# An inner Strassen level on four of the seven products of an output stage

What was changed: the last stage of a gated mixer kernel is a matrix product that already uses one level of Strassen's scheme. In three quarters of it, four of the seven products are split once more, and the attention output that feeds the stage is kept in fp16 instead of bf16. (Strassen's scheme makes a product of 2 x 2 blocks from seven block products in place of eight, at the price of sums of blocks before and after.)

## The chip, the cores and the metric

One core of a Trainium2 chip. The metric is the device time of one execution in microseconds (us), the median over several executions. Verdicts use ±2% as "same"; 95% intervals stand beside the ratios. The engines are PE (TensorE), PEld (its weight loads), DVE (VectorE), ACT (ScalarE), POOL (GpSimd) and SP (SyncE, which issues the DMA transfers here). PSUM (`psum_all` in the profile) is the memory that PE's matmuls write and that DVE and ACT read (L435 `psum_all<-arena`, 2425 matmuls before; L1297 on DVE, L296 on ACT: `arena<-psum_all`); the kernel uses it in pieces that it calls banks. `arena` is the kernel's buffer space.

## The reference, cut to what matters

```python
x = A_x                                                  # 1 x 2048 x 1024, bf16
g = sigmoid((x * gate_w).sum(-1, keepdims=True))
# A: attention over 8 positions at a distance of 2, 32 heads; then  o @ wo     (1024 -> 1024)
# B: gelu(x @ w_in), a spatial product over the sequence, then      (z1*gs) @ w_out   (1792 -> 1024)
return g * A + (1 - g) * B
```

The gate is folded into the two activations earlier in the kernel, so both final products are one contraction of 1792 + 1024 = 2816 = 22 chunks of 128 (14 gated gMLP chunks, 8 attention chunks), for 16 tiles of 128 tokens by 1024 columns. That contraction is the output stage.

## The kernel before: the parts that matter

Five helpers carry the argument: a product into a PSUM bank, the seven Strassen steps (a generator, so that steps can be interleaved), the loads of activations, their sums, and one "quad" (two token tiles by two column halves of 512, with 2 x 11 chunks).

```python
def product(bank, pairs, start, N=512):                         # L435: the matmuls
    n = len(pairs)
    for m, (lhsT, rhs) in enumerate(pairs):
        nc.tensor.matmul(bank[:, 0:N], lhsT, rhs, start=(start and m == 0), stop=(m == n - 1), ...)

def strassen(A11, A12, A22, S1, S2, S3, S4, B11, B21, B22, T1, T2, T3, T4, vs, c11, c12, c21, c22, ...):
    # ... bank roles X, Y, Z, V; bookkeeping cut
    product(X, pairs(A11, B11), True, N);  nc.scalar.copy(Y[:, n], X[:, n]);   yield
    product(V, pairs(S1, T1), True, N);    share(vs, V[:, n]);                 yield
    product(Y, pairs(S2, T2), False, N);   nc.scalar.copy(Z[:, n], Y[:, n]);   yield
    product(X, pairs(A12, B21), False, N); c11(X);                             yield
    product(Y, pairs(S3, T3), False, N)
    seed = nc.scalar.copy(V[:, lo], Y[:, lo]); c22(Y);                         yield
    product(Z, pairs(S4, B22), False, N);  c12(Z);                             yield
    # ... the last step in two halves for the last quad, cut
    product(V, pairs(A22, T4), False, N);  c21(V);                             yield

def load_act(i):
    d = act_slots[i % 3]
    for a in range(2):
        row = i + 8 * a
        for x in range(2):
            src = zg_d[row][:, NFH * x * P:NFH * (x + 1) * P].rearrange("p (k t) -> p k t", t=P)
            sync.dma_start(d[F16][x][:, 0:NFH, a, :], src)                     # 7 gated chunks, fp16
            sync.dma_start_transpose(d[BF][x][:, NFH:KOH, a, :], o_d[...])     # 4 attention chunks, bf16

def out_quad(i):
    # ... slots cut
    for k0, k1, dt in ((0, NFH, F16), (NFH, KOH, BF)):                         # sums split by type
        t = d[dt]
        sums4([s[q][:, k0:k1, :] for q in range(4)], t[0][:, k0:k1, 0], t[1][:, k0:k1, 0], ...)
    # ... c11, c12, c21, c22: copy or add into the output buffer and store
    run(strassen(A(0, 0), A(1, 0), A(1, 1), ...))

# the stage
out_sums_late()                   # the last of the weight sums
load_act(1)
for i in range(8):                # eight quads, one after the other
    if i + 2 < 8:
        load_act(i + 2)
    out_quad(i)
```

## Time and profile before

| | before |
|---|---|
| time, median of 3 (a fourth run came later) | 665.98 us (665.54 to 666.79) |
| PE busy, share of the span | 99% |
| output stage, first to last matmul | 526.6 to 659.8 us: 133.2 us |
| the same in halves (matmuls of 256 columns, a 512 counts as two) | 1232 |

How to read what follows. A page of the profile names groups of instructions by source line and engine, "out<-in". A timeline row is: start, length, engine, line, operation, "out<-in", count, and in brackets the idle time of that engine just before, with what ended it. A row of the chain of waits is: start, length, what. The lines of the kernel before that carry the bound are in the prediction.

### The profile page before, as it was taken

The page shows a single profiled execution, that of the slowest core. Times are in us where ns is not written, and L with a number is a line of the kernel's source. Part 1 is how long each engine was busy: PE and PEld are TensorE (multiplying, and loading weights), DVE is VectorE, ACT ScalarE, POOL GpSimd, SP SyncE. Part 2 cuts the span into 40 slices and gives each one's busy share as a digit, 9 for nine tenths or more (in the row PEclk, how much of TensorE's full clock was granted, in tenths as well). Part 3 has the DMA queues.
Part 4 walks back from the last instruction along what each step waited for, and adds up shares of the span by engine and source line. Part 5 has one row for each costly group of instructions (what it writes and reads, how often), then busy time and mean ns, then how long its engine had stood idle before and what let it go on. Part 6 is the DMA issues. An engine that isn't in the chain of part 4 may idle for free.

```text
span 662.9 us, 10747 instructions
## 1 busy us (share of the span) xinstructions
PE 656.5 (99%) x4194; PEld 316.7 (48%) x4194; DVE 451.8 (68%) x671; ACT 294.4 (44%) x621; POOL 6.2 (1%) x15
## 2 busy tenths in 40 slices
PE   9999999999999999999999999999999999999998
PEld 4544467444454555444444444444444444444444
DVE  2520889978998999898868766887679853333301
ACT  4544676565587577799653111121121122222221
POOL 1000000000000000001000000000000000000000
PEclk9999999999999999999999999999999999999999
DMA  9988663797585050259974568479645789533000
GB/s 217 185 211 224 130 152 90 189 217 188 129 202 162 1 155 1 64 159 250 236 214 157 128 158 168 119 212 279 97 121 142 163 176 214 120 96 98 32 33 33
DMA packets 229475, 98.16 MB, mean 148 GB/s; under 512 B 177440, under 2 KB 215728, under 8 KB 229424
## 3 DMA queue, kind: packets, MB, share of 16 engines
q1 hardware_dynamic: 229136, 97.27, 61.0%
q8 instruction: 33, 0.54, 0.4%
q10 hardware_dynamic: 288, 0.20, 0.1%
q14 instruction: 18, 0.15, 0.1%
HBM read 45.10 MB, written 36.61 MB: 123 GB/s over the span
## 4 chain that ended last, share of the span: by engine, by line
PE 96%; ACT 2%; DVE 1%; DMA 1%; issue 0%; ACTq 0%
PE psum_all L435 72%; PE psum_all L293 17%; PE psum_all L303 3%; PE psum_all L355 2%; DMA att_L<-band_d 1%; ACT arena L815 1%; PE psum_all L318 1%; ACT arena L363 0%; PE psum_all L491 0%; DVE arena L708 0%; DVE psum_all L506 0%; PE psum_all L225 0%; PE psum_all L822 0%; ACT L815 0%; DVE arena L713 0%
## 5 line engine op out<-in xcount | busy, mean ns | idle before, releaser
L435 PE MATMUL psum_all<-arena 128*128 128x512 bf16 (+5 forms) x2425 | 495.9, 367 | 1.3 <-DVE psum_all L506 1.2
L435 PEld LDWEIGHTS <-arena 128*128 128x128 f16 (+1 forms) x2425 | 237.1, 98 | 258.9 <-issue 2.7
L293 PE MATMUL psum_all<-arena 128*128 128x512 bf16 x512 | 114.8, 379 | 0.0
L293 PEld LDWEIGHTS <-arena 128*128 128x128 bf16 x512 | 48.5, 98 | 56.2 <-issue 0.2
L708 DVE TENSOR_TENSOR arena<-arena,att_A 128x2048 f16<-128x2048 bf16 (+1 forms) x44 | 73.3, 1705 | 0.3
L296 ACT CAST arena<-psum_all 128x512 bf16<-128x512 f32 x64 | 37.3, 586 | 50.9 <-PE psum_all L293 50.9
L581 DVE TENSOR_TENSOR arena<-arena 128x1024 f16<-128x1024 f16 (+3 forms) x31 | 18.9, 610 | 47.1 <-PE psum_all L435 36.2
L453 ACT COPY psum_all<-psum_all 128x512 f32<-128x512 f32 (+1 forms) x30 | 15.8, 527 | 76.8 <-PE psum_all L435 73.0
L815 ACT ACTIVATE arena<-psum_all 128x448 bf16<-128x448 f32 x64 | 34.1, 546 | 19.4 <-DVE psum_all L506 9.8
L1095 ACT ACTIVATE arena<-psum_all 128x512 bf16<-128x512 f32 x56 | 31.5, 600 | 20.9 <-PE psum_all L435 13.9
L506 DVE TENSOR_TENSOR psum_all<-psum_all,arena 128x448 f32<-128x448 f32 (+1 forms) x58 | 37.3, 661 | 4.5 <-PE psum_all L435 3.6
L583 DVE TENSOR_TENSOR arena<-arena 128x1024 f16<-128x1024 f16 (+3 forms) x31 | 18.7, 608 | 30.9 <-PE psum_all L435 17.7
L712 DVE TENSOR_TENSOR arena<-arena 128x2048 f16<-128x2048 f16 (+1 forms) x22 | 37.2, 1704 | 0.1
L477 ACT COPY psum_all<-psum_all 128x512 f32<-128x512 f32 (+2 forms) x30 | 15.6, 522 | 46.2 <-PE psum_all L435 45.2
L363 ACT CAST arena<-psum_all 128x1988 f16<-128x1988 f32 (+3 forms) x25 | 33.9, 1357 | 1.2 <-PE psum_all L355 0.4
L459 ACT COPY arena<-psum_all 128x512 f32<-128x512 f32 (+1 forms) x30 | 16.2, 544 | 36.9 <-PE psum_all L435 33.1
L464 ACT COPY psum_all<-psum_all 128x512 f32<-128x512 f32 (+1 forms) x30 | 15.9, 528 | 36.3 <-PE psum_all L435 35.6
L870 ACT ACTIVATE arena<-arena 128x896 bf16<-128x896 bf16 x32 | 30.4, 959 | 0.0
L582 DVE TENSOR_TENSOR arena<-arena 128x1024 f16<-128x1024 f16 (+3 forms) x31 | 18.4, 609 | 10.4 <-PE psum_all L435 10.3
L1297 DVE TENSOR_TENSOR arena<-psum_all,arena 128x512 bf16<-128x512 f32 x8 | 5.5, 691 | 29.3 <-ACT psum_all L477 29.3
L303 PE MATMUL psum_all<-arena 128*128 128x385 bf16 x128 | 23.0, 331 | 0.0
L584 DVE TENSOR_TENSOR arena<-arena 128x1024 f16<-128x1024 f16 (+3 forms) x31 | 18.5, 605 | 2.9 <-PE psum_all L435 2.9
(95 smaller groups left out, 404.6 us busy)
## 6 DMA issues: line engine op xcount, KB each, us to landing
arena<-v_d SPq DMA_DIRECT2D x8, 960.0 KB, 6.2
z_d<-arena SPq DMA_DIRECT2D x14, 512.0 KB, 4.7
arena<-z_d SPq DMA_DIRECT2D x14, 512.0 KB, 4.4
zg_d<-arena SPq DMA_DIRECT2D x56, 128.0 KB, 2.2
arena<-zg_d SPq DMA_DIRECT2D x32, 224.0 KB, 3.2
band_d<-arena SPq DMA_DIRECT2D x28, 248.5 KB, 4.6
arena<-in_A_wqkv_dram SPq DMA_DIRECT2D x16, 256.0 KB, 4.4
o_d<-arena SPq DMA_DIRECT2D x4, 1024.0 KB, 6.3
```

Source lines behind the costliest of these rows:

```text
L293: nc.tensor.matmul(ps[:], w[:, t, kt, :], xT[:, kt, 512 * c:512 * (c + 1)], start=(kt == 0), stop=(kt == KT - 1))
L296: nc.scalar.copy(dst[:, :, 256 * c:256 * (c + 1)], ps[:].rearrange("p (n e) -> p e n", e=2))
L303: nc.tensor.matmul(ps[:, 0:VP + 1], xT[:, kt, i * P:(i + 1) * P], wvp[:, kt, :], start=(kt == 0), stop=(kt == KT - 1))
L363: nc.scalar.copy(dst, src)
L435: nc.tensor.matmul(bank[:, 0:N], lhsT, rhs, start=(start and m == 0), stop=(m == n - 1), skip_group_check=True)
L506: last_add[0] = nc.vector.tensor_tensor(out[:, n], a[:, n], vs, ALU.add)
L581: first = nc.vector.tensor_tensor(s_out[0], a21, a22, ALU.add)
L708: lambda ws=ws, in0=in0, in1=in1: tt(p5[:, ws], in0[:, ws], in1[:, ws], ALU.mult)), False
L712: lambda a=p3[:, ws], b=p3[:, ws.start + 4:ws.stop + 4]: tt(a, a, b, ALU.add)), not n
L815: nc.scalar.activation(z2[:, i + 8 * a, ZC * c:ZC * (c + 1)], bank[:, 0:ZC], ACT.Gelu_apprx_tanh, accum_out=s1[:, 4 * n + c:4 * n + c + 1])
L870: return nc.scalar.activation(junk, src, ACT.Square, accum_out=(s2, s2h)[x][:, n:n + 1])
L1095: last_gelu[0] = nc.scalar.activation(z1s[:, f, a, :], bank[:], ACT.Gelu_apprx_tanh)
```

## The change

Intent: take matmul time out of a stage that is nothing but matmuls. Quads 0 and 1 stay. The other six are done two at a time (a "pair"); four of a pair's seven products (numbered 1, 7, 4 and 2) become Strassen products of two token tiles by 2 x 256 columns over ten of the eleven chunks, the eleventh plain, in two rounds of two interleaved products; the other three products (`rest`) stay plain. DVE pays with sums of weights and activations. The diff, cut to its core:

```diff
-    o_d = dpool.tile([S, D], BF, name="o_d")
+    o_d = dpool.tile([S, D], F16, name="o_d")
 ...
-        for k0, k1, dt in ((0, NFH, F16), (NFH, KOH, BF)):
-            t = d[dt]
-            sums4([s[q][:, k0:k1, :] for q in range(4)], ...)
+    def act_sums(i):
+        sums4(so_slots[i], *[act_block(i, x, a) for a in range(2) for x in range(2)])
 ...
+    raw_in = {xa: pair_slot(R_OFF + 22528 + 2 * SQ * n) for n, xa in enumerate(((0, 0), (1, 0), (0, 1), (1, 1)))}
+    a_of = {1: raw_in[0, 0], 4: raw_in[1, 0], 7: raw_in[1, 1], 2: s_in[0]}
+    def load_block(q, x, a):                       # two loads, each followed by a transposing load
+        d = raw_in[x, a]
+        for i in range(2):
+            load_tokens(2 * q + i + 8 * a, x, d[:, 0:NFH, i, :], d[:, NFH:KOH, i, :])
+    def pair_sum(q): ...                           # L1368: an outer sum, 2816 elements
+    def inner_sums(n, last=True, first=True):
+        ...
+            tt(s[:, 0], a21, a22, ALU.add)         # L1374, 640 elements
+            tt(s[:, 1], s[:, 0], a11, ALU.subtract)
+            tt(s[:, 2], a12, s[:, 1], ALU.subtract)
+            tt(a21, a11, a21, ALU.subtract)        # L1378
+    def inner(side, n, put):                       # mm: matmuls of 256 columns, L1391
+        mm(X, part(0, 0), w.b11, True);                 nc.scalar.copy(Y[:, h], X[:, h])        # L1397
+        mm(V, [s[:, 0, k] for k in k5], w.t1, True);    nc.scalar.copy(vs, V[:, h])
+        mm(Y, [s[:, 1, k] for k in k5], w.t2);          tt(Z[:, h], Y[:, h], vs, ALU.add)       # L1405
+        mm(X, part(KI, 0), w.b21, False, 0, 0);         put(0, 0, X[:, h])
+        mm(Y, part(0, 1), w.t3);                        tt(V[:, h], Y[:, h], vs, ALU.add)       # L1412
+        mm(Z, [s[:, 2, k] for k in k5], w.b22, False, 0, 1);   put(0, 1, Z[:, h])
+        mm(Y, part(KI, 1), w.t4, False, 1, 0);  mm(V, [], [], False, 1, 1)
+        put(1, 1, V[:, h]);  put(1, 0, Y[:, h])
+        # (a yield after each step cut)
+    def rest(q, m): ...                            # products 3, 5, 6, plain; adds and stores
+    def out_pairs():
+        for q in (1, 2, 3):
+            more = q < 3
+            run(inner(0, 1, keep_first), inner(1, 7, add_first(kept[2])))
+            ...
+            if more:
+                for xa in ((1, 1), (0, 1), (0, 0)):
+                    load_block(q + 1, *xa)
+            run(inner(0, 4, to_out(q)), inner(1, 2, add_first(kept[1])))
+            if more:
+                load_block(q + 1, 1, 0)
+                pair_sum(0)
+                inner_sums(7)
+            ...                                    # rest, with the other sums between its steps
 ...
-    load_act(1)
-    for i in range(8):
-        if i + 2 < 8:
-            load_act(i + 2)
-        out_quad(i)
+    for xa in ((1, 1), (0, 1), (0, 0), (1, 0)):
+        load_block(1, *xa)
+    act_sums(0)
+    out_quad(0, {})
+    ...                                            # inner weight sums, the first pair's sums, out_quad(1)
+    out_pairs()
```

The program text is not the order on an engine: a scheduler sets that when the kernel is built. The prediction read the built order.

## The prediction

> **What bounds the kernel now.** I read the page's busy shares and slices first, then the chain that ended last, then groups by shape in the output stage, then timelines of ScalarE, VectorE and the DMA queue around that stage's start.
>
> ```profile
> span 662.9 us, 10747 instructions
> ...
> PE 656.5 (99%) x4194; PEld 316.7 (48%) x4194; DVE 451.8 (68%) x671; ACT 294.4 (44%) x621; POOL 6.2 (1%) x15
> ...
> PE   9999999999999999999999999999999999999998
> ...
> DVE  2520889978998999898868766887679853333301
> ...
> PEclk9999999999999999999999999999999999999999
> ```
> TensorE (PE) is busy throughout at full clock; VectorE (DVE) is nearly full until slice 32 and then has two thirds free. The last eight slices are the output stage, the only one the change touches apart from some sums and loads made just ahead of it.
>
> The chain of waits from 370 us on, in order of time (start, length, what):
> ```profile
> 369.92 287.49 PE psum_all L435 x1332
> 657.41 2.42 PE psum_all L491 x22
> 659.82 0.02 issue
> 659.85 0.42 DVE arena L1314
> ```
> So 290 us of unbroken matmuls end the kernel: nothing is waited for, 1332 matmuls take 287.49 us, 0.2158 each, and 22 of 256 columns take 2.42, 0.110 each. Any matmul time removed here is won whole, and any bubble made here is lost whole.
>
> Where the stage begins, from ScalarE's timeline:
> ```profile
> 529.24 0.57 ACT L453 COPY psum_all<-psum_all 128x512 f32<-128x512 f32 x1 [5.20 <-PE psum_all L435]
> 531.62 0.59 ACT L459 COPY arena<-psum_all 128x512 f32<-128x512 f32 x1 [1.80 <-PE psum_all L435]
> 533.99 0.57 ACT L464 COPY psum_all<-psum_all 128x512 f32<-128x512 f32 x1 [1.79 <-PE psum_all L435]
> ```
> Steps are 2.37 us apart (11 matmuls of 0.2158). The first product ends at 529.0, so the stage starts at 526.6 and its matmuls end at about 659.8: 133.2 us for eight quads of 7 x 11 matmuls. I count in halves (256 columns): 8 x 154 = 1232 halves, 0.1081 each.
>
> DVE durations that I use, from its groups by shape:
> ```profile
> L1174 DVE TENSOR_TENSOR arena<-arena 128x2048 f16<-128x2048 bf16 x14 | 17.1, 1218 | 0.0
> ...
> L1303 DVE TENSOR_TENSOR arena<-psum_all,arena 128x512 bf16<-128x512 f32 x8 | 5.5, 691 | 3.2 <-PE psum_all L435 3.2
> ...
> L581 DVE TENSOR_TENSOR arena<-arena 128x512 f16<-128x512 bf16 x8 | 3.4, 426 | 1.9 <-PE psum_all L435 1.5 <-DMA arena<-o_d 0.4
> ...
> L1314 DVE CAST arena<-psum_all 128x256 bf16<-128x256 f32 x1 | 0.4, 425 | 1.7 <-PE psum_all L491 1.7
> ```
> 2048 16-bit elements take 1.22 us and 512 take 0.43: 0.52 ns an element over about 0.15 us; PSUM reads take 0.69 us for 512, 0.42 for 256. In a back-to-back run successive starts lie some 0.08 us closer than that (2048 elements: 1.13 us).
>
> The DMA queue when it only loads activations (each fp16 load followed by a transposing load of attention output):
> ```profile
> 540.84 0.53 SPq L190 DMA_DIRECT2D arena<-zg_d  x1
> 541.46 1.20 SPq L195 DMA_TRANSPOSE arena<-o_d  x1
> 542.71 0.57 SPq L190 DMA_DIRECT2D arena<-zg_d  x1
> 543.34 1.24 SPq L195 DMA_TRANSPOSE arena<-o_d  x1
> ```
> One load and one transpose take 1.87 us of the queue; for the transposes issue to landing is 2.7/3.1/3.4 us (min/median/max) between 560 and 610 us.
>
> [...]
>
> **The change part by part.** Token-tile quads 0 and 1 stay as they were (308 halves). The other six are done in three pairs. In each pair, four of the seven products become an inner Strassen over 2 token tiles by 2 x 256 columns: seven products of five chunks, and the eleventh chunk plain: 7 x 5 + 4 = 39 halves in place of 2 x 11 x 2 = 44. Five halves saved, times four products, times three pairs: 60 halves. The stage goes to 308 + 3 x 288 = 1172 halves.
> Matmul time removed: 60 x 0.1081 = 6.5 us.
> Matmul time added: 3 x (156 + 44) = 600 of the matmuls are now 256 wide, each about 1 ns dearer than half of a 512 (0.109 against 0.108): +0.6 us. Net -5.9 us. The tail stays: last matmul, one DVE pass over 256 columns, one 64 KB store.
> fp16 attention output: same bytes. The activation sums no longer split by type, so quads 0 and 1 need 4 DVE instructions each in place of 8. Free.
>
> VectorE work, which used to be hidden: (a) sixteen sums of 1280 elements for the inner weights, about 0.8 us each; (b) per pair, four sums of 2816 elements (1.6 us) and sixteen of 640 (0.48). Between the spatial stage's last additions and the first pair this is 3.4 (the late weight sums) + 16 x 0.74 + 16 x 0.40 + 4 x 1.53 + 4 x 0.60 = 30 us of DVE by start-to-start times, to be done while TensorE does quads 0 and 1, which take 33.3 us. DVE also comes late from the spatial stage (I add up its order to about 529.7) and, in that order, the first inner sum waits for the first pair's activations. These may only be loaded when the last gated spatial result has been stored (issued at about 532, landed at 534); block one is two loads and two transposes, 3.7 us of queue plus 3.2 to land: 541. DVE gets there at about 537.4 and so idles 3.6 us. From 541 on I add the order up: the first addition of the first inner product starts at about 564.8. TensorE reaches the step that needs it (eight products in, 4.6 us after 559.9) at 564.5; with two additions of 0.42 it goes on at about 565.3. Loss 0.8 us by this sum; sliding later is likelier than sooner: I put +1.3.
>
> The dearest part is a matter of order. In the second inner round of pairs 1 and 2, three inner sums of the *next* pair stand in DVE's queue, and the first of them ahead of the round's first two PSUM additions. It reads activations whose slot is freed only as the first inner round ends (call it t). Then: 0.25 us to the queue, load, transpose, load, transpose, the last issued at t+2.8, landed at t+5.5 to 6.0; the sum 0.48, the addition 0.42: t+6.5 to 7.0. TensorE needs the addition before product 9 of the round (six of 5 halves, two of 6), at t+4.6. Bubble: about 2.2 us, twice: +4.4 us. The third pair has no successor, so no such wait.
>
> Sum: 666.0 - 6.5 + 0.6 + 1.3 + 4.4 = 665.8. Between pairs the order leaves the last pair sum and the first addition with next to no slack but no wait by my count; I leave that at zero. I take 665.5, a shade below, because the two bubbles are built from median landing times in a busier queue.
>
> **The rivals.** First, everything hides: then 666.0 - 5.9 = 660.1. For it: DVE's last slices show 3 tenths, transposes land in 2.7 us at best, and the weight load fits. Against: the DVE sum of 30 us in 33, and a DMA wait seen in the order ahead of urgent additions. Second, VectorE becomes the bound of the first two quads: if loading begins 3 us later than I think, as the full DMA (9 tenths around 527 to 553) allows, all of it appears at the first pair: 668 to 669. Third, 256-wide matmuls pay for weight loads when mixed with semaphore waits (98 of 109 ns leaves little): at 115 ns each, 600 x 6 ns = +3.6 us, 669. The clean run of 22 speaks against it. Fourth, the two DVE bubbles are smaller because loads are issued sooner: 661 to 663.
>
> **Range and chances.** The saving is bounded at 5.9 us, and the bubbles are 0 to 5 (first pair) and 2 to 6 (the two rounds). Predicted 665.5 us, 661.5 to 669.0 eight times in ten. 2% is 13.3 us: the whole matmul saving is under half of that, and a loss of that size needs 19 us of bubbles. Faster by over 2%: 0.01; within 2%: 0.97; slower by over 2%: 0.02.
>
> **What would show it.** Right: the output stage has about 1172 halves and runs of 256-wide matmuls with 109 ns spacing; PE shows gaps on DVE releasers of about 2 us in the second inner round of pairs 1 and 2 and none in pair 3; DVE's first inner sum there waits for a transpose or a load landing some 5.5 us after the round begins; DVE is 9 tenths busy during quads 0 and 1, with one wait for a load near 537 to 541 us. Wrong: no PE gap (then 660), a spacing above 112 ns, gaps in the plain third parts of the pairs, or a lower clock.

The matmul figures that the terms and the third rival use can be read from the trace before: the 22 matmuls of 256 columns (L491) fill 2.56 us, the last of them 0.272, so they start (2.56 - 0.272) / 21 = 0.109 us apart; a weight load (L435 on PEld) takes 98 ns. Two premises of the second-round term were not shown by that trace and were assumptions: that a DVE instruction which waits holds back those behind it, and the 0.25 us to the queue. For both, the trace of the changed kernel has a measured number, given in the result: a wait of 3.27 us with two additions behind it, and 0.20 us.

## More of the kernel before

One more view is needed for later: the busy time of each engine in the stage's first two stretches of two quads each. The columns are the stretch and its length, then busy us and (instructions) of PE, PEld, DVE, ACT and POOL, the granted TensorE clock (PEclk), the busy share of the DMA engines and GB/s:

```profile
526.60:559.90 33.30, 33.30 (x156) 15.09 (x154) 17.04 (x33) 6.35 (x11) 0.00 (x0) 1.00 0.94 199
559.90:593.10 33.20, 33.20 (x155) 15.05 (x154) 10.99 (x20) 6.94 (x12) 0.00 (x0) 1.00 0.49 109
```

PE is full in both; DVE has half of the first and two thirds of the second free. Two quads take 33.2 us.

## The result

| | before | changed |
|---|---|---|
| time, median of 4 runs each | 665.97 us (665.54 to 666.79) | 661.46 us (659.77 to 661.73) |
| ratio | | 0.9926 [0.9906, 0.9945]: same |

Ratios here are the mean time of one kernel's fast runs over the mean of the other's fast runs of the same rounds, so not quite the ratio of the medians.

The gain is 4.5 us, and 661.46 lies just under the low end of the predicted range, 661.5. The profiled run of the changed kernel took 659.77 us and is the fastest of its four; the other three (661.2 to 661.73) left no profile. The page of the changed kernel:

```profile
span 657.9 us, 11379 instructions
...
PE 650.5 (99%) x4453; PEld 341.3 (52%) x4453; DVE 503.2 (76%) x762; ACT 290.0 (44%) x632; POOL 6.2 (1%) x15
...
DVE  2520889978999999898778676887659999595952
```

DVE is busy for 51 us more, and its last eight slices, 53333301 before, now read 99595952. TensorE is still the bound.

The chain of waits, which before was one line of 287 us, now has other pieces in it (start, length, what):

```profile
559.59 9.54 PE psum_all L1391 x88
569.13 2.91 DMA arena<-o_d
...
572.54 0.44 DVE psum_all L1405
...
573.02 4.09 PE psum_all L1391 x36
...
623.55 17.03 PE psum_all L1391 x156
640.58 14.31 PE psum_all L435 x88
```

The last two lines are the third pair: 156 halves take 17.03 us (0.109 each), 88 matmuls of the plain part 14.31 (44 of 512 columns, 44 of 256), together 31.3 us in place of 33.2. The lines above show the second inner round of the first pair: it waits for a transposing load of attention output, then for an addition on DVE. In TensorE's timeline these are its only gaps in the stage:

```profile
573.02 4.09 PE L1391 MATMUL psum_all<-arena 128*128 128x256 f16 x36 [0.33 <-DVE psum_all L1405]
605.16 4.09 PE L1391 MATMUL psum_all<-arena 128*128 128x256 f16 x36 [0.66 <-DVE psum_all L1405]
```

So they are where the prediction put them, in the second round of pairs 1 and 2 and not in pair 3, but they measure 0.99 us together instead of 4.4. DVE's timeline has the wait that causes the first of them:

```profile
537.92 0.49 DVE L1374 TENSOR_TENSOR arena<-arena 128x640 f16<-128x640 f16 x1
...
562.43 0.98 DVE L1405 TENSOR_TENSOR psum_all<-psum_all,arena 128x256 f32<-128x256 f32 x2 [1.11 <-PE psum_all L1391]
...
572.13 0.49 DVE L1374 TENSOR_TENSOR arena<-arena 128x640 f16<-128x640 f16 x1 [3.27 <-DMA arena<-o_d]
572.54 0.76 DVE L1405 TENSOR_TENSOR psum_all<-psum_all,arena 128x256 f32<-128x256 f32 x2
```

At 572.13 the sum L1374 has kept DVE waiting for 3.27 us, and the two additions that TensorE needs stand behind it. The first line (537.92) is the first inner sum of the first pair: it has no bracket, so DVE did not wait for that pair's activations. The second line shows DVE ready 1.11 us ahead of TensorE at the first addition, so nothing was lost there.

The DMA queue's timeline says why the wait is short:

```profile
528.68 2.06 SPq L190 DMA_DIRECT2D zg_d<-arena  x4
530.90 0.41 SPq L190 DMA_DIRECT2D arena<-zg_d  x1
...
563.77 0.38 SPq L190 DMA_DIRECT2D arena<-zg_d  x1
566.61 1.80 SPq L195 DMA_TRANSPOSE arena<-o_d  x1
...
569.13 1.20 SPq L195 DMA_TRANSPOSE arena<-o_d  x1
```

The first inner round runs from 559.43 and ends 78 halves later, at 567.95. The block for the next pair is loaded into the slot that this round still reads, but its first load is issued at 563.77, while the round is half done and 4.2 us before it ends, and the last of its four transfers at 569.13, only 1.2 us after the round's end (the prediction had 2.8).

The order of the round's matmuls, read from the code, gives these times. The slot holds two token tiles of 11 chunks. The first load writes chunks 0 to 6 of tile 0; the last matmul that reads one of them is number 38 of 78 (chunk 6, in the fourth step of product 7), at 559.43 + 38 x 0.109 = 563.57. The transposing load behind it writes chunks 7 to 10 of tile 0; chunk 10 is read last by matmul 64, at 566.41. The queue issues them 0.20 us after each of these. The other two follow as the queue gets to them, at 568.50 and 569.13. In this stage the queue's rows for single transposing loads are 1.19 to 1.25 us long for 20 of the 24 (1.28 to 2.14 for the other four, 1.80 at 566.61 among them), those for the plain loads between them 0.38 to 0.58 us for 23 of the 24 (1.40 for one).

One measure serves the experiments, since the stages ahead of this one scatter: the *stage time*, from ScalarE's first seed copy of the output stage (L453, the copy of bank X into Y in the first Strassen step) to the start of the last DVE pass behind the last matmul. Before: 529.24 to 659.85, 130.6 us. Changed: 528.76 to 654.92, 126.2 us.

### The profile page after: what moved, and what is told of

It is laid out like the page before. It is cut to its first block, busy times and chain, and to the rows that moved or that the text cites. A ratio compares the mean times of both kernels' runs of the same rounds, so it can differ in the third digit from the quotient of the medians.

```text
span 657.9 us, 11379 instructions
## 1 busy us (share of the span) xinstructions
PE 650.5 (99%) x4453; PEld 341.3 (52%) x4453; DVE 503.2 (76%) x762; ACT 290.0 (44%) x632; POOL 6.2 (1%) x15
## 4 chain that ended last, share of the span: by engine, by line
PE 95%; ACT 2%; DMA 2%; DVE 1%; issue 0%; SPq 0%; DVEq 0%; ACTq 0%
PE psum_all L435 66%; PE psum_all L293 17%; PE psum_all L1391 7%; PE psum_all L303 3%; PE psum_all L355 2%; DMA arena<-o_d 1%; DMA arena<-in_A_x_dram 1%; ACT arena L815 1%; ACT arena L363 0%; SPq L162 0%; PE psum_all L822 0%; DVE arena L708 0%; DVE psum_all L506 0%; ACT L815 0%; PE psum_all L225 0%
## 5 line engine op out<-in xcount | busy, mean ns | idle before, releaser
L435 PE MATMUL psum_all<-arena 128*128 128x512 f16 (+6 forms) x2238 | 442.0, 360 | 0.7 <-DVE psum_all L506 0.6
L435 PEld LDWEIGHTS <-arena 128*128 128x128 f16 (+1 forms) x2238 | 218.8, 98 | 222.2 <-issue 2.2
L1391 PE MATMUL psum_all<-arena 128*128 128x256 f16 (+1 forms) x468 | 51.9, 273 | 1.0 <-DVE psum_all L1405 1.0
L1391 PEld LDWEIGHTS <-arena 128*128 128x128 f16 x468 | 45.8, 98 | 6.8 <-issue 1.3
L453 ACT COPY psum_all<-psum_all 128x512 f32<-128x512 f32 (+1 forms) x24 | 12.4, 517 | 67.4 <-PE psum_all L435 66.6
L477 ACT COPY psum_all<-psum_all 128x512 f32<-128x512 f32 (+1 forms) x24 | 12.4, 518 | 37.0 <-PE psum_all L435 36.0
L581 DVE TENSOR_TENSOR arena<-arena 128x1024 f16<-128x1024 f16 (+2 forms) x17 | 12.2, 720 | 19.5 <-PE psum_all L435 15.7
L464 ACT COPY psum_all<-psum_all 128x512 f32<-128x512 f32 (+1 forms) x24 | 12.4, 518 | 25.6 <-PE psum_all L435 24.8
L459 ACT COPY arena<-psum_all 128x512 f32<-128x512 f32 (+1 forms) x24 | 12.7, 532 | 24.9 <-PE psum_all L435 22.5
L671 DVE TENSOR_TENSOR att_m<-att_L 128x256 f16<-128x256 f16 x8 | 2.3, 288 | 23.8 <-DMA att_L<-band_d 23.8
L713 DVE TENSOR_TENSOR arena<-arena 128x2048 f16<-128x2048 f16 x16 | 19.5, 1221 | 0.3
```

Of the source, the lines that this page charges most:

```text
L1391: nc.tensor.matmul(bank[:, h], l, r, start=(start and m == 0), stop=(m == len(ab) - 1), skip_group_check=True)
```

## The experiments

Ten kernels ran, in three batches, each batch on one chip with the kernel before run beside it; all ten gave correct results. Two theories are told apart:

- The working of the prediction: loads come late (at the round's end; behind the last store of the spatial stage), which costs 4.4 and 1.3 us.
- Its rival: loads are issued piece by piece as parts of a slot come free, so little is lost.

The table gives all of them; "gaps" are TensorE's idle times in the output stage of the profiled run, in order. Where no number of runs stands, there were 5.

| kernel | median us (range, runs) | ratio to before [95%] | stage time | gaps us |
|---|---|---|---|---|
| a0, changed, order fixed | 661.02 (659.90 to 663.16, 6) | 0.9945 [0.9931, 0.9959] | 126.1 | 0.74 |
| e1, sums behind the round | 660.28 (659.59 to 660.37) | 0.9928 [0.9916, 0.9940] | 125.5 | 0.30 |
| e2, round loads late | 663.69 (663.49 to 664.00) | 0.9981 [0.9968, 0.9994] | 128.9 | 1.72, 1.67 |
| e3, first load late | 663.27 (660.75 to 664.27, 6) | 0.9969 [0.9953, 0.9985] | 127.5 | 0.49, 0.50, 0.71 |
| e7, sums inside the round | 659.92 (659.57 to 661.74, 6) | 0.9926 [0.9913, 0.9939] | 125.8 | 0.61 |
| e5, pairs without inner Strassen | 665.26 (663.78 to 665.44) | 0.9994 [0.9982, 1.0006] | 130.7 | none |
| e6, before with fp16 alone | 665.41 (664.24 to 666.57, 6) | 1.0004 [0.9989, 1.0018] | 130.6 | none |
| e4, both loads late | 665.94 (665.55 to 666.99) | 1.0011 [0.9999, 1.0023] | 131.7 | 0.49, 1.91, 2.11 |
| e8, no sum waits ahead of a PSUM read | 659.03 (658.40 to 659.70) | 0.9907 [0.9893, 0.9921] | 124.9 | none |
| a1, changed, order fixed, again | 661.39 (659.06 to 662.39, 6) | 0.9935 [0.9918, 0.9953] | 125.5 | 0.40 |

The first four are one batch (before: 665.2), the next four the second (665.18), the last two the third (665.48).

### a0: the control

Changing one dependency would let the scheduler reshuffle other instructions. So each variant of the changed kernel but e5 has DVE's order in the stage written down. a0 writes down the order as it is, and no instruction moves:

```diff
     out_pairs()
     settle()
+    as_is = (5064, 5065, 5066, ...)            # VectorE's instructions of the stage, as built
+    found = {i.name: i for i in nc.cur_bb.bb.instructions}
+    for a, b in zip(as_is, as_is[1:]):
+        tc.add_manual_dep(found[f"I-{b}"], f"I-{a}", NOSYNC, reason="VectorE's order as it was")
```

> The changed kernel again, with VectorE's order in the output stage written down as it already is (no instruction moves on any engine), as the reference for the three runs beside it. All theories: 4.5 us under the kernel before (661.5 against 666.0), two gaps on TensorE of 0.3 to 0.7 us in the second inner rounds of pairs 1 and 2, and no others in the output stage.

It is the changed kernel: 661.02 against 661.46 us. Its profiled run was the slowest of six (663.16), with a stage time of 126.1 like the first. It shows one gap (0.74, pair 2) where two were expected; a1 below shows one as well (0.40, pair 1), so these gaps vary from run to run. What made that run slower happened 330 us earlier, in the attention stage, which the change does not touch. TensorE's timeline there, and in a second fence the busy times and the clock of a stretch shortly behind:

```profile
199.89 6.38 PE L435 MATMUL psum_all<-arena 128*128 128x448 f16 x24 [2.29 <-DVE psum_all L506]
```

```profile
202.00:204.00 2.00, 2.00 (x7) 0.88 (x6) 0.89 (x2) 1.43 (x5) 0.00 (x0) 0.50 0.37 33
```

After a gap of 2.29 us the granted clock fell to 0.50, and PE got through 7 matmuls in these 2 us, where in the other runs looked at it did 12 or 13. Eight gaps of over 1 us were found on TensorE from 5 us on in the twelve profiles. Behind one other, of 2.11 us (e4, below), the granted clock was 0.50 as well; behind the other six, 1.20 to 1.91 us long (before, e2, e3, e4), it was 1.00. The slow stretch in the attention stage is why the stage time, not the total, carries the verdicts below.

### e1: the waiting sums behind the round

The three inner sums (L1374, L1375, L1376) move behind the second round's last addition, so that no instruction that waits for a load stands ahead of a PSUM addition in that round.

```diff
-  ... 1374, 1405, 1405, 1375, 1468, 1376, 1462, 1412, 1412, 1468, 1462, 1468, 1468, 1462, 1462, 1368
+  ... 1405, 1405, 1468, 1462, 1412, 1412, 1468, 1462, 1468, 1468, 1462, 1462, 1374, 1375, 1376, 1368
```

(Line numbers in DVE's order, second round of pairs 1 and 2.)

> The three inner sums of the next pair that stand in and ahead of the second round's PSUM additions are put behind that round's last addition; nothing else moves on any engine, the loads stay as they are. Theory (VectorE's order makes the gaps: an urgent addition stands behind a sum that waits for a transposing load): both gaps go, the output stage has none, 1.0 us faster than the changed kernel (660.5). Rival (TensorE itself lacks the late activations or weights, the order is beside the point): the gaps stay at 0.3 and 0.7 us, and the time stays at 661.5.

Both gaps are gone, so the wait for the load ahead of the additions was their cause, and the stage is 0.6 us shorter than a0's: a new gap, which the expectation did not have, came in at the start of pair 2's first round.

```profile
594.70 15.22 PE L1391 MATMUL psum_all<-arena 128*128 128x256 f16 x136 [0.30 <-ACT psum_all L1397]
```

ScalarE's copy (L1397, at 594.96) there waits 0.31 us for DVE's late addition L1445 of the pair before, which reads PSUM until 594.87. That the moved sums pushed this addition back is not shown: e7 takes them away from there, and the gap grows. DVE had also waited for transposing loads in the part before it (0.61 us ahead of 582.20 and 0.88 ahead of 587.51), more than the 0.30 that TensorE lost; e7 and e8 take this up.

### e2: the prediction's premise made true

The first load of the next pair waits for the last matmul of the first round. The prediction assumed that the slot comes free only then. DVE's order is fixed as in a0.

```diff
-                nc.tensor.matmul(bank[:, h], l, r, ...)
+                last_mm[0] = nc.tensor.matmul(bank[:, h], l, r, ...)
...
-                    load_block(q + 1, *xa)
+                    load_block(q + 1, *xa, behind=last_mm[0] if xa == (1, 1) else None)
```

> The premise of the prediction made true: the first load of the next pair's first block may only be issued when TensorE has ended the first inner round (in pairs 1 and 2); VectorE's order as in the changed kernel. Theory (the prediction's mechanism was right, its premise that the slot is freed as a whole at the round's end was wrong; piece by piece release lets the last transpose be issued 1.2 to 1.5 us after the round's end in place of 2.8): the last transpose is issued about 2.8 us after the round's end, lands at 5.8, and the gaps grow from 0.33 and 0.66 to about 2.0 us each; 3.0 us slower than the changed kernel (664.5). Rival (the prediction's landing and addition times were too long, the moment of issue mattered little): gaps of under 1 us each and under 1 us slower.

TensorE's gaps, and in a second fence the last transposing load in the DMA queue:

```profile
575.41 4.09 PE L1396 MATMUL psum_all<-arena 128*128 128x256 f16 x36 [1.72 <-DVE psum_all L1410]
608.94 4.09 PE L1396 MATMUL psum_all<-arena 128*128 128x256 f16 x36 [1.67 <-DVE psum_all L1410]
```

```profile
571.48 1.26 SPq L195 DMA_TRANSPOSE arena<-o_d  x1
```

(L1396 and L1410 are L1391 and L1405 of the changed kernel, moved down by the edit.) The first round ended at 568.96 here, so the last transposing load is issued 2.5 us behind it, near the predicted 2.8, and the two gaps are 3.39 us together against 0.74 in a0; the stage is 2.8 us longer than a0's, and 4.1 us longer than e8's (below), which has no gap; the prediction had put 4.4. The mechanism of the prediction is right here, and its size follows the time at which the slot comes free. The rival (under 1 us slower) is out: 2.7 us in the median.

### e3: the first pair's loads late

The first load for the first pair waits for the last late weight sum on DVE, which brings it to 536.77, 5.6 us behind the stage's first seed copy; the prediction's 534 was 4.8 us behind that of before (529.24), so this is rather later than predicted.

```diff
-        load_block(1, *xa)
+        load_block(1, *xa, behind=last_late[0] if xa == (1, 1) else None)
```

> The prediction's other premise made true: the first pair's first load waits until VectorE has ended the late weight sums (about 534.3 us in place of 530.9); VectorE's order as in the changed kernel. Theory (VectorE had 1.1 us to spare before the first inner product's addition, and 1.4 us more until TensorE needs it): VectorE idles about 2.5 us around 538 to 543 us, the first inner round gets a gap of 0 to 0.5 us, and the time rises by as much. Rival (VectorE bounds the first two quads): the 2.5 us show whole as a gap at the first round, 664.

DVE's first inner sum and TensorE's first round:

```profile
542.40 0.49 DVE L1381 TENSOR_TENSOR arena<-arena 128x640 f16<-128x640 f16 x1 [1.98 <-DMA arena<-o_d]
...
567.31 8.68 PE L1398 MATMUL psum_all<-arena 128*128 128x256 f16 x78 [0.49 <-DVE psum_all L1412]
```

(The edit moves the lines down by seven: L1381, L1398 and L1412 here are L1374, L1391 and L1405 of the changed kernel.) DVE waits 1.98 us for this load and 0.87 for the next, 2.85 in all, and TensorE loses 0.49 in the first round, where a0 and the changed kernel lose nothing. The profile answers the question. The time does not: it rose by 2.2 us, more than this gap, in a kernel whose six runs scatter over 3.5 us. Its total is inconclusive: in the profiled run the output stage itself began 2.4 us later than the changed kernel's (531.15 against 528.76), behind two gaps of 1.25 and 1.50 us in the attention stage. (The other two gaps are the two of the changed kernel.)

### e7: the sums inside the round

A better place was sought for the three sums: behind the two additions L1412, one between each of the additions that follow.

```diff
-  ... 1374, 1405, 1405, 1375, 1468, 1376, 1462, 1412, 1412, 1468, 1462, 1468, ...
+  ... 1405, 1405, 1468, 1462, 1412, 1412, 1374, 1468, 1375, 1462, 1376, 1468, ...
```

> The order experiment again, but the three sums stay inside the second inner round, one by one behind the two additions that free the last bank, where TensorE no longer waits for VectorE; nothing else moves. Theory (the new 0.3 us gap of the order experiment at the start of pair 2 came from 1.2 us of sums pushed into a part where VectorE is full, so that a copy there waited for a late PSUM read): no gap at either second round and none at the start of pair 2; the stage, from its first ScalarE copy to the last matmul, 125.2 us (126.2 in the changed kernel, 125.5 in the order experiment); time 660.0. Rival (that gap has another cause, for instance the loads): it stays at 0.3 us, 660.3.

The gaps of the second rounds are gone again, and again there is one gap at the start of pair 2:

```profile
593.83 15.23 PE L1391 MATMUL psum_all<-arena 128*128 128x256 f16 x136 [0.61 <-ACT psum_all L1397]
```

DVE's timeline shows that no lack of time made it:

```profile
586.64 0.49 DVE L1374 TENSOR_TENSOR arena<-arena 128x640 f16<-128x640 f16 x1 [1.91 <-DMA arena<-o_d]
```

This is an inner sum of another product (number 4, in the plain part), which waits for the last block's transposing load and stands ahead of the PSUM reads L1439, L1440 and L1445. The same pattern as in the second rounds, one part later. So this experiment's theory (too much work on DVE) failed, and its rival (the loads) fits: TensorE lost 0.61 us where DVE had waited 1.91. The stage, 125.8 us, is no shorter than e1's 125.5.

### e5: the pairing without the inner products

The pairs, the loads and the outer sums stay; the four inner products are plain again, and the inner sums are gone.

```diff
-        mm(X, part(0, 0), w.b11, True)
-        ...                                     # the seven inner steps
+        for m, bank in ((0, X), (1, V)):
+            product(bank, [(a[:, k, m], w.full[k]) for k in KH], True)
+            put(m, 0, bank[:, h])
+            put(m, 1, bank[:, NI:2 * NI])
+            yield
```

> One part undone: the pairs stay, with their pair sums, loads and bank plan, but the four inner Strassen products are plain products again (two token tiles by 512 columns, 11 chunks), and the inner sums of weights and activations go with them. Theory (the gain is the matmul time of 60 halves, 6.5 us, less 0.5 for width, and nothing else in the change moves the time): 1232 halves, stage 130.6 to 131.2 us as in the kernel before, no gaps, time that of the kernel before within 0.5 us (ratio 0.999 to 1.001). Rival (pairing, the later out-weight sums or the single-typed activations bring part of the gain): clearly under the kernel before, ratio 0.997 or less.

TensorE's timeline of the stage is one line without a gap, and the time is that of before:

```profile
529.64 130.91 PE L435 MATMUL psum_all<-arena 128*128 128x512 f16 x663
```

So the pairing itself costs and gives nothing that these runs can tell (0.9994 [0.9982, 1.0006]): the gain comes with the removed halves.

### e6: the fp16 attention output alone, in the kernel before

```diff
-    o_d = dpool.tile([S, D], BF, name="o_d")
+    o_d = dpool.tile([S, D], F16, name="o_d")
...
-        for k0, k1, dt in ((0, NFH, F16), (NFH, KOH, BF)):
+        for k0, k1, dt in ((0, KOH, F16),):
```

> The other part alone: the kernel before with attention output kept in fp16, so that the activation sums of the output stage are no longer split by type; no inner products. Theory: the same time as the kernel before (ratio 0.999 to 1.001), VectorE about 1 us less busy in the output stage, no gap on TensorE anywhere in it. Rival (a share of the gain is the type): ratio 0.998 or less.

Same time, same stage. DVE's busy time in the stage falls from 42.2 to 38.1 us, more than the 1 us expected, and none of it is on the path.

### e4: both premises made true

e2 and e3 together. If the prediction's own premises hold, its own time should come out.

> Both false premises of the prediction made true at once (first load of pair 1 after the late weight sums, first load of pairs 2 and 3 only when the inner round has ended), VectorE's order as in the changed kernel. Theory (the prediction's sum failed in these two terms and nowhere else): gaps of 0.5 us in the first round and 1.7 us in each of two second rounds, 3.9 us in all against 1.0 in the changed kernel; stage 129.1 us, time about 664.0, which is near the predicted 665.5. Rival (something else in the sum was off by microseconds): stage under 128 or over 131 us.

The total is 665.94, next to the predicted sum of 665.8, but that is partly luck. TensorE's timeline, and in a second fence the clock behind the last gap:

```profile
575.52 4.09 PE L1398 MATMUL psum_all<-arena 128*128 128x256 f16 x36 [1.91 <-DVE psum_all L1412]
609.12 5.73 PE L1398 MATMUL psum_all<-arena 128*128 128x256 f16 x36 [2.11 <-DVE psum_all L1412]
```

```profile
609.10:610.50 1.40, 1.38 (x7) 1.01 (x7) 1.40 (x5) 0.00 (x0) 0.00 (x0) 0.50 0.74 169
```

The three gaps sum to 4.51 us, where 3.9 was expected and the prediction's terms are 5.7. After the gap of 2.11 us the clock was granted at 0.50, and the 36 halves behind it took 5.73 us instead of 4.09: 1.64 us that neither theory had. By the letter the rival's mark (a stage over 131 us) is met: the stage took 131.7, or 130.1 without this slow stretch. Four of the five runs show the same mean clock (0.997); the fifth, at 1.000, still took 665.55, so the clock is not all of the luck.

### e8 and a1: no sum that waits ahead of a PSUM read

e7, and the inner sums of product 4 move as well: from the plain part to behind the two additions L1412 of the next pair's first round. On DVE 64 positions differ from the changed kernel's; on TensorE, ScalarE and in the DMA queue none.

```diff
   # e7's order, and in addition, for pairs 2 and 3:
-  ... the sums of product 4 (1374, 1375, 1376, 1378) among 1439, 1440, 1445
+  ... 1412, 1412, 1374, 1375, 1376, 1378      # behind the first round's additions
```

> The mid-round order, and in addition the four inner sums of the pair's last activation block (pairs 2 and 3) are taken from in front of the PSUM reads of the plain part and put into the next first round, behind its two freeing additions; loads and TensorE's order unchanged. Theory (all gaps left have one form: a sum that waits for a transposing load, in front of a PSUM read in VectorE's queue): no gap on TensorE in the output stage at all, stage (first ScalarE copy to last matmul) 125.2 us against 126.2 in the changed kernel and 125.8 in the mid-round one, time 659.5. Rival (VectorE has too much work in the plain part, whatever the order): a gap of 0.3 us or more stays at the start of pair 2 or 3, stage 125.5 or more.

> The changed kernel once more, beside the run above on the same chip, to compare them directly: 661.2 us by the two earlier measurements, one or two gaps of 0.3 to 0.8 us in the second inner rounds, stage 126.2 us. Theory and rival agree here.

e8's chain of waits for the first and second pair, back to back:

```profile
559.50 17.03 PE psum_all L1391 x156
576.54 14.30 PE psum_all L435 x88
590.84 17.03 PE psum_all L1391 x156
```

No gap is left. The stage time is 124.85 us, 5.76 less than before's 130.61: the matmul saving in full. The median, 659.03, is 2.4 us under the changed kernel's on the same chip (661.39) and 6.4 under before's, so this has the shortest stage of all, and it beats the changed kernel in a direct comparison. Not settled is why the total won 2.4 us. The two profiled runs, 659.06 (a1, its fastest) and 658.40 (e8, its fastest), differ by 0.66, just as their stages do (125.52 and 124.85); the rest lies in a1's other five runs (660.19 to 662.39), which left no profile. The changed kernel's runs scatter over 3.3 us here and e8's over 1.3.

## Why the prediction was wrong, point by point

It gave 665.5 us (661.5 to 669.0); measured 661.46. The class, same within 2%, was right, as the size of the possible saving made certain.

- **The matmul term (-6.5 + 0.6 = -5.9) held.** Each pair takes 31.3 us where two quads took 33.2, three times 1.9, or 5.7. The 256-wide spacing is 0.109 us (156 in 17.03), as assumed. e8, with no gap left, shows 5.76; e5, with the inner products undone, and e6, with the type alone, show no gain from anything else.
- **The second-round term (+4.4) was mis-sized: it measured 0.99, 0.74 and 0.40** in three profiles of the changed kernel. (These are the gaps in the timeline. By the stage time, against e8's 124.85, the three lost 1.3, 1.3 and 0.7 us. In e8, where nothing stops, a round shows 17.19 us but the next matmul starts after 17.03; where TensorE stops, we estimate that this 0.16 us is lost besides the gap. In a0, pair 2's first 120 matmuls also show 13.60 us in place of 13.26.) The step that failed is "It reads activations whose slot is freed only as the first inner round ends". The slot comes free in pieces, and the queue had issued the loads of half of it before the round ended (at 563.77 and 566.61 against 567.95): the last transposing load came at t+1.2 (t is the end of the first inner round) instead of t+2.8, and landed at t+4.1 (572.04) instead of t+5.5 to 6.0. With the premise made true (e2), the gaps are 3.4 us and the stage is 4.1 us longer than e8's. The rest of this step held: the engine, the lines, the two pairs, and the third pair without a wait.
- **The first-pair term (+1.3) measured 0.** The step that failed is "These may only be loaded when the last gated spatial result has been stored (issued at about 532, landed at 534)". The last of those stores were issued by 530.7, and the first load followed at 530.90, without waiting for them to land (their median from issue to landing is 2.3 us, and the last was issued at 530.2). DVE reached its first inner sum at 537.92 (predicted 537.4) and found the data there. With the load held back (e3), DVE idles 2.85 us and TensorE 0.49, so even with its premise (and a load somewhat later than that) this term was too large.
- **The DVE count held.** About 30 us of sums in 33 were predicted for quads 0 and 1; DVE was busy 33.1 of 33.2 us and ready 1.11 us before TensorE at the first addition.
- **The range was cut too high at its low end.** It allowed 0 to 5 us for the first bubble but 2 to 6 for the other two, so the failed premise was also the floor. The fourth rival, "the two DVE bubbles are smaller because loads are issued sooner: 661 to 663", is what happened, and a floor near 0 for the two bubbles would have followed from it.
- **Two rivals were answered.** Matmuls of 256 columns did not pay for weight loads (0.109 us in runs of 156, with weight loads of 98 ns, L1391 on PEld), and DVE did not become the bound of the first two quads. The first rival, that everything hides (660.1), did not hold for the changed kernel but nearly names what a better order gives: e8, 659.03.

With the terms as measured, 666.0 - 5.8 + 0 + 1.3 (by the stage time) gives 661.5, beside 661.46. That it fits so closely is partly luck, since the runs of the changed kernel scatter over 2 us and the 1.3 comes from the fastest of them.

One reading of the prediction was loose, and nothing rests on it: VectorE was not "nearly full" until slice 32; from slice 5 on its line shows 6 to 9 tenths.

## What to carry to other kernels

When a load waits for a buffer, ask which part of the buffer each transfer writes and which instruction reads that part last, and count it in the order of the reader; here "free when the round ends" was 4.2 us too late for the first load (563.77 against 567.95). In the built order of DVE, keep an instruction that waits for a load behind the PSUM reads that others need (here a wait of 3.27 us on DVE stood ahead of two additions, and TensorE lost 0.33), and look for the next such place when one is removed: here there were two. Judge a change of under 1% by the time of the stage that it touches, beside the total: two profiled runs of the changed kernel (the first one and a0) have stage times of 126.2 and 126.1 us and totals of 659.77 and 663.16.
